# Attention through 32 packed rows, then a gated MLP: another stored order and another split of the first stage's work over the engines

## The chip, the cores and the metric

The kernel runs on one core of a Trainium2 chip. A core has five engines with their own in-order instruction queues: TensorE (PE, matmuls), VectorE (DVE), ScalarE (ACT), GpSimd (POOL) and SyncE (SP, which here only issues DMAs). The metric is the device time of one execution in microseconds, as the median of several runs.

## The reference

Eight batches, eight heads, 576 tokens of 64 features; all in fp32, with the tolerance of an fp32 result.

```python
def sm_attn(qq, kk, vv):
    s = scale * np.matmul(qq, kk.transpose(0, 1, 3, 2))
    s = s - np.max(s, axis=-1, keepdims=True)
    a = np.exp(s)
    a = a / (np.sum(a, axis=-1, keepdims=True) + 1e-09)
    return np.matmul(a, vv)
p_packed = sm_attn(p, k, v)           # 32 packed rows per head
out = sm_attn(q, p_packed, p_packed)  # every token attends to these 32 rows
...
rms = np.sqrt(np.mean(x * x, axis=-1, keepdims=True) + 1e-06)
xn = x / rms * rms_g                  # 4608 tokens x 512
g = xn @ w_gate                       # 512 -> 1536
silu = g * (1.0 / (1.0 + np.exp(-g)))
val = xn @ w_val
return (silu * val @ w_out)           # 1536 -> 512
```

## The kernel before, in words

[...] To come out at fp32 accuracy every operand is split into a high and a low fp16 part that are multiplied separately and summed in PSUM.

**The stages.** The 4608 tokens go through in 12 units of 384. For each batch, the rows p attend to k and v (stage 1: keys transposed on PE at L865 and evicted at L869, scores at L1031 and L1038, exponentials at L957, transposes evicted at L1073, packed values at L1116). Then q attends to the packed rows (queries L1426, L1431; scores L1492; softmax L1513 to L1526; the weights transposed at L1358 and split into a high part by L1378 on ACT and a low part by L1380 on DVE, the tile `aTu`). The output of attention is not formed by itself: the packed rows are multiplied into the gate and value weights ahead of time ("packed weights": L1218, L1268 and L1270 scale, L1287 multiplies, L536 and L538 split the result into the ring buffer), and L1693 multiplies `aTu` by them. That gives gate and value of a unit, 12 chunks of 128 features each. The norm's factors come as a per-chunk scale `usc` from L1668. L1729 applies silu on ACT, L1732 the product on DVE, L1744 casts the high part of the result, L1747 subtracts for the low part, both into `hall`; L1720 multiplies by w_out, and the result is evicted (L1767 on ACT, L1769 on DVE) and stored.

**The weights.** All weights are loaded once, in 12 pieces of gate and value (L614) and 6 of w_out (L673), 1 MB each, in the first 80 us, into raw buffers that are parts of `ring`, `wo` and `hall`. Each piece is taken apart into two arrays by `to_f32`: L573 on ACT makes one result; the low part is then made by L578 on POOL, L580 on ACT or L582 on DVE; L587 (or L585, where DVE made the low part) on DVE combines. The maxima for the scaling of the pieces are found by matmuls (L640 for gate/val, L691 for w_out), reduced by L645 or by L695 (DVE) or L697 (ACT), and turned into scales by L658 to L660, L720. Then w_out is split: L750 on ACT (high part), L752 on DVE (low part) and L755 (a copy of the high part).

**What sets the order.** The program is a number of generators ("chains"): keys, v, stage 1, the 18 weight pieces, queries, attention, packed weights, the MLP and so on. Each `yield` names an engine and the step's assumed cost, and each step then issues its instructions. A class `Plan` runs one step at a time in the order that the table `ORDER` (L43, 2805 numbers of chains) gives; so `ORDER` fixes the order in every engine's queue and in the DMA queue of SP. `FETCHES` (L58) is a list of assumed latencies with which TensorE's instructions are fetched; it goes into the plan's own times, by which it places filler matmuls (L1801, whose results are not used) where it thinks that PE would stand idle, and into which free buffer it takes. `BY` (L334) says by one letter per step which engine does it: A for ACT, D for DVE, P for POOL. A step that may go to several engines asks `way`:

```python
by, step = way(table, i, {"P": (POOL, 1.07, t0), "A": (ACT, act(n) + 0.06, t0), "D": (DVE2, 0.61, t1)})
yield step
if by == "P":
    nc.gpsimd.tensor_scalar(lo, lo.bitcast(U8)[..., 3::4], 1 / 32, -15.5 / 32, ALU.mult, ALU.add)
elif by == "A":
    nc.scalar.activation(lo, lo.bitcast(U8)[..., 3::4], AF.Copy, scale=1 / 32, bias=-15.5 / 32)
else:
    nc.vector.tensor_single_scalar(d, d, 3, ALU.logical_shift_left)
```

The tables of `BY` that matter here: `low` and `low_wo` (L578, L580 or L582, of the 12 and of the 6 pieces), `norm_wo` (L695 or L697), `wo_hi` (L755), `lo0` (L1747 of the first unit), `hi0` (L1744 of the first unit), `scaled` (L1643 on ACT or L1645 on DVE), `pgv` (L1268 on ACT or L1270), `keys` (L869), `a1t` (L1073).

## Time and profile before

| | before |
|---|---|
| median of 3 runs | 735.23 us (734.9 to 736.16) |
| profiled execution | 735.44 us, span 733.7 us |
| PE busy | 712.3 us (97%) |
| DVE busy | 469.6 us (64%) |
| ACT busy | 460.9 us (63%) |
| POOL busy | 138.6 us (19%) |
| granted clock of TensorE, mean | 0.991 of full speed |

The shares of the whole span are a mean over two very different parts: the first 120 us, in which the weights are loaded and taken apart while the first unit is computed, and the rest, in which the units follow each other. The page's strip of 40 slices shows the two parts; one slice is 18.3 us:

```profile
PE   8888999999999999999999999999999999999997
...
DVE  3898897788968767667657747656455553561330
ACT  4698996887797665777488477377274364461330
POOL 1235211111442242220020021020020040020110
PEclk9799999999999999999999999999999999999999
DMA  7996513677607741415734763631330333301001
```

A digit is a tenth of the slice in which the engine was busy (9 for 90% or more); PEclk is the clock granted to TensorE and DMA the share of the 16 DMA engines.

### The profile page before, as it was taken

To read this page: it belongs to the slowest core of one execution; us is meant where nothing else is said; L and a number is where in the kernel's file an instruction comes from. 1 tells how busy PE (TensorE), PEld (TensorE's weight loads), DVE (VectorE), ACT (ScalarE), POOL (GpSimd) and SP (SyncE) were. 2 spreads that over 40 slices of the span, in tenths; PEclk is the share of its full clock that TensorE was granted. 3 is DMA by queue.
4 is the path that set the end of the run, shared out by engine and by line. 5 is a ranking of instruction groups with operands and counts; after the bars stand their busy time and mean duration, and the time that the engine had idled before them with its cause. 6 is when DMAs were issued, how large, how long until landed. Compare 5 with 4: busy or idle time off the path is not lost.

```text
span 733.7 us, 19223 instructions
## 1 busy us (share of the span) xinstructions
PE 712.3 (97%) x8052; PEld 427.8 (58%) x8052; DVE 469.6 (64%) x1063; ACT 460.9 (63%) x964; POOL 138.6 (19%) x157
## 2 busy tenths in 40 slices
PE   8888999999999999999999999999999999999997
...
DVE  3898897788968767667657747656455553561330
ACT  4698996887797665777488477377274364461330
POOL 1235211111442242220020021020020040020110
PEclk9799999999999999999999999999999999999999
DMA  7996513677607741415734763631330333301001
GB/s 284 388 379 230 198 34 67 119 188 139 174 5 116 185 130 16 108 46 96 187 90 78 160 165 63 150 80 22 72 81 15 80 81 58 88 2 37 15 0 58
DMA packets 143239, 82.25 MB, mean 112 GB/s; under 512 B 105392, under 2 KB 128432, under 8 KB 143152
## 3 DMA queue, kind: packets, MB, share of 16 engines
...
q8 instruction: 63, 1.03, 0.6%
...
## 4 chain that ended last, share of the span: by engine, by line
PE 82%; DMA 7%; DVE 4%; ACT 3%; SPq 3%; issue 1%; POOL 0%; ACTq 0%; DVEq 0%
PE pm_1x L1720 12%; PE pm_3x L1693 10%; PE pm_1x L1693 9%; PE pm_2x L1693 9%; PE pm_2x L1720 9%; PE pm_0x L1693 8%; PE pm_0x L1720 8%; PE pm_3x L1720 7%; DMA wo<-in_moe_w_gate_dram 2%; DMA wo<-in_moe_w_val_dram 2%; SPq L614 2%; PE psa L1499 1%; DMA ring<-in_moe_w_out_dram 1%; PE pm_2x L1299 1%; DMA big_3x<-big_1x 1%
## 5 line engine op out<-in xcount | busy, mean ns | idle before, releaser
L1693 PEld LDWEIGHTS <-ring 128*128 128x128 f16 x2304 | 204.1, 98 | 86.0 <-issue 13.8
L1720 PEld LDWEIGHTS <-hall 128*128 128x128 f16 x1296 | 124.0, 98 | 148.5 <-issue 4.9
L1720 PE MATMUL pm_1x<-wo,hall 128*128 128x512 f16 x432 | 97.3, 379 | 0.6 <-ACT wo L755 0.6
L1747 POOL TENSOR_TENSOR hall<-t_1x,hall 128x384 f16<-128x384 f32 x44 | 41.2, 937 | 255.8 <-ACT hall L1744 250.6
L1720 PE MATMUL pm_3x<-wo,hall 128*128 128x512 f16 x288 | 64.8, 379 | 0.0
L1720 PE MATMUL pm_2x<-wo,hall 128*128 128x512 f16 x288 | 64.3, 379 | 0.0
L1720 PE MATMUL pm_0x<-wo,hall 128*128 128x512 f16 x288 | 64.1, 379 | 0.0
L1747 POOL TENSOR_TENSOR hall<-t_0x,hall 128x384 f16<-128x384 f32 x31 | 29.8, 962 | 162.9 <-ACT hall L1744 150.5
L1744 ACT CAST hall<-t_0x 128x384 f16<-128x384 f32 x69 | 35.1, 509 | 22.7 <-DVE t_0x L1732 22.4
L1693 PE MATMUL pm_3x<-aTu_1x,ring 128*128 128x192 f16 (+1 forms) x354 | 49.2, 283 | 0.0
L1693 PE MATMUL pm_1x<-aTu_0x,ring 128*128 128x192 f16 (+1 forms) x342 | 45.8, 278 | 0.3 <-ACT t_1x L1729 0.2
L1744 ACT CAST hall<-t_1x 128x384 f16<-128x384 f32 x67 | 34.0, 508 | 18.7 <-DVE t_1x L1732 18.7
L1693 PE MATMUL pm_2x<-aTu_1x,ring 128*128 128x192 f16 (+1 forms) x324 | 45.8, 284 | 0.0
L1693 PE MATMUL pm_3x<-aTu_0x,ring 128*128 128x384 f16 (+1 forms) x270 | 43.4, 301 | 1.0 <-ACT t_0x L1729 0.6
L1693 PE MATMUL pm_0x<-aTu_0x,ring 128*128 128x192 f16 (+1 forms) x276 | 38.9, 284 | 1.1 <-ACT t_1x L1729 0.9
L1693 PE MATMUL pm_0x<-aTu_1x,ring 128*128 128x192 f16 (+1 forms) x264 | 36.7, 283 | 0.0
L1693 PE MATMUL pm_2x<-aTu_0x,ring 128*128 128x192 f16 (+1 forms) x264 | 36.6, 282 | 0.0
L1693 PE MATMUL pm_1x<-aTu_1x,ring 128*128 128x384 f16 (+1 forms) x210 | 33.1, 299 | 0.0
L1747 DVE TENSOR_TENSOR hall<-t_0x,hall 128x384 f16<-128x384 f32 x42 | 24.7, 587 | 4.9 <-ACT hall L1744 4.7
L1320 POOL TENSOR_TENSOR wgv<-o_0x,wgv 128x512 f16<-128x512 f32 x14 | 16.9, 1210 | 46.8 <-ACT wgv L1318 46.8
L1729 ACT ACTIVATE t_0x<-pm_2x,usc_1x 128x384 f32<-128x384 f32 x12 | 7.0, 581 | 26.3 <-PE pm_2x L1693 23.0
L538 DVE SCALAR_TENSOR_TENSOR ring<-pm_1x,ring 128x512 f16<-128x512 f32 x24 | 16.5, 687 | 9.1 <-ACT ring L536 9.0
...
## 6 DMA issues: line engine op xcount, KB each, us to landing
...
hall<-in_moe_w_out_dram SPq DMA_DIRECT2D x4, 1024.0 KB, 10.0
wo<-in_moe_w_gate_dram SPq DMA_DIRECT2D x3, 1024.0 KB, 15.1
wo<-in_moe_w_val_dram SPq DMA_DIRECT2D x3, 1024.0 KB, 13.7
...
ring<-in_moe_w_gate_dram SPq DMA_DIRECT2D x2, 1024.0 KB, 9.1
ring<-in_moe_w_val_dram SPq DMA_DIRECT2D x2, 1024.0 KB, 12.4
```

The lines of the kernel that those rows point to most:

```text
L538: nc.vector.scalar_tensor_tensor(lo, x, s, hi, ALU.mult, ALU.subtract)
L614: nc.sync.dma_start(raw.rearrange("p k n e -> p k (n e)"), (w_gate, w_val)[n][:, 4 * c * P : 4 * (c + 1) * P].rearrange("(kt p) f -> p kt ...
L1299: nc.tensor.matmul(ps[e][32 * j : 32 * j + 32, :], pg[h, lp, j, :], wgv16[h, c, j, lw, :], start=(n3 == 0), stop=(n3 == 2),)
L1320: nc.gpsimd.tensor_tensor(wgv16[:, c, k, 1], st, wgv16[:, c, k, 0], ALU.subtract)
L1499: nc.tensor.matmul(ps2[o : o + n, i, :, pi, :], qT[:, lq, i, pi, o : o + n], packs[b][3][:, lp, pi, :, :], start=(j == 0), stop=(j == 2),)
L1693: nc.tensor.matmul(psi[:, :, o : o + n], pw[:, g, lw, w, f * P : (f + 1) * P], aT[:, :, la, g, o : o + n], start=(j == 0), stop=(j == 5),)
L1720: nc.tensor.matmul(po, hall[:, ft, lh, ts], wo[:, ft, 1 - lw, :], start=(n == 0), stop=(n == 3 * NFT - 1))
L1729: nc.scalar.activation(t, pss[0][:, :UT], AF.Silu, scale=sc[:, c, 0:1])
L1744: (nc.scalar.copy if by == "A" else nc.vector.tensor_copy)(hall[:, ft, 0, :], t)
L1747: (nc.gpsimd if by == "P" else nc.vector).tensor_tensor(hall[:, ft, 1, :], t, hall[:, ft, 0, :], ALU.subtract)
```

## The change

Three tables are replaced: `ORDER`, `FETCHES` and `BY`; no function is changed. Of the 63 entries of `FETCHES` some 50 differ; `ORDER` has the same length and differs from entry 17 on. `BY` in full, and the first entries of the other two:

```diff
-ORDER = (0, 0, 0, 0, 0, 0, 0, 0, 0, 0, 0, 0, 0, 0, 0, 0, 0, 0, 0, 0, 34, 34, 34, 35, 35, 35, 34, 1, 16,
+ORDER = (0, 0, 0, 0, 0, 0, 0, 0, 0, 0, 0, 0, 0, 0, 0, 0, 0, 16, 16, 3, 4, 3, 0, 1, 0, 0, 34, 34, 34, 35,
...
-FETCHES = (8.0, 8.0, 8.0, 8.0, 8.0, 8.0, 6.7276, 6.7063, 4.3, 4.3, 8.5735, 8.8308, 9.7613, 7.0833,
+FETCHES = (8.0, 8.0, 8.0, 8.0, 8.0, 8.0, 8.0, 4.6203, 4.3, 4.3, 9.1414, 6.3883, 7.3965, 7.163,
...
-BY = {'low': 'ADPAAAADAPAP', 'low_wo': 'APAPDP', 'pgv': 'DAPAAPDAPAAPDAPAAP', 'norm_wo': 'AADADA',
-  'keys': 'DAADADDDDADA', 'query': 'AAADDA', 'hi0': 'DADDDAADDDAD', 'lo0': 'DPDDPDDPDPPP',
-  'gv': 'PDDDPP', 'wo_hi': 'AAAAAP', 'a1t': 'DDDDAD', 'scaled': 'AAAAAA', 'store': 'DDDDDD
+BY = {'low': 'DPPPAPAAPPPP', 'low_wo': 'PPPPPP', 'pgv': 'PPDAPAPPPAAPDAPAAP', 'norm_wo': 'DDDDDD',
+  'keys': 'AADAADAAAADA', 'query': 'ADDAAA', 'hi0': 'ADDDDDADAAAA', 'lo0': 'PPPPPPPPPPPP',
+  'gv': 'DPDPPD', 'wo_hi': 'PPPPPP', 'a1t': 'DADAAA', 'scaled': 'DDADDA', 'store': 'ADDDDD
...
```

In the whole program ACT loses six L580 (9 to 3), all four L697, all five L755, four L1268 and four L1643, and gains four L869 and three L1073; DVE loses six L1747, three L1073, four L869, two L582 and others, and gains four L695 and four L1645; POOL gains eight L578 (6 to 14), six L1747, five L755 and three L1270. PE has the same matmuls in nearly the same order, with 31 fillers for 33: a run of twelve next to L647 is gone, others stand ahead of L1067, L1116 and later. In SP's queue the loads of q, of the norm's gain and of the first gate piece now stand ahead of v; the weight pieces keep their order among themselves.

Three places of the order follow. The first is POOL around the first scales `usc` (L1668). `wo_79`, `ring` and `hall` are the raw buffers: the first row is the last gate/val piece, the following L578 are w_out's. Before:

```order
L578 TENSOR_SCALAR wo_79<-wo_79 128x1024
L1668 TENSOR_SCALAR usc_0x<-gv_sc,tiny_18x 128x2
L578 TENSOR_SCALAR ring<-ring 128x1024
L1668 TENSOR_SCALAR usc_0x<-gv_sc,tiny_18x 128x2
L1270 TENSOR_TENSOR pgh_1x<-pg_0x,gv_r 128x256
L658 TENSOR_SCALAR gv_sc<-tiny_21x,gmax 128x1
L659 TENSOR_SCALAR gv_sc<-gv_r,gmax_r 128x1
L660 TENSOR_SCALAR wo_sc<-tiny_21x,gsq 128x1
L1668 TENSOR_SCALAR usc_0x<-gv_sc,tiny_18x 128x2 x2
L578 TENSOR_SCALAR hall<-hall 128x1024
L1747 TENSOR_TENSOR hall<-t_1x,hall 128x384
```

and now:

```order
L578 TENSOR_SCALAR wo_79<-wo_79 128x1024
L578 TENSOR_SCALAR hall<-hall 128x1024
L1668 TENSOR_SCALAR usc_0x<-gv_sc,tiny_19x 128x2
L658 TENSOR_SCALAR gv_sc<-tiny_21x,gmax 128x1
L659 TENSOR_SCALAR gv_sc<-gv_r,gmax_r 128x1
L660 TENSOR_SCALAR wo_sc<-tiny_21x,gsq 128x1
L578 TENSOR_SCALAR ring<-ring 128x1024
L1668 TENSOR_SCALAR usc_0x<-gv_sc,tiny_19x 128x2
L578 TENSOR_SCALAR hall<-hall 128x1024 x2
L1747 TENSOR_TENSOR hall<-t_1x,hall 128x384
L1668 TENSOR_SCALAR usc_0x<-gv_sc,tiny_19x 128x2
```

The first scales stood behind the last gate/val piece alone and now stand behind the first w_out piece too; the third stood ahead of w_out's fourth piece and now stands behind its third and fourth.

The second place is ACT between the last gate/val piece (L573 into `wgv`) and the first silu. Before:

```order
L1643 ACTIVATE e_0x<-e_0x,trio_3x 128x256 x3
L1431 COPY big_1x<-pm_0x 128x512
L1268 ACTIVATE pgh_0x<-pg_0x,gv_r 128x128 x2
L573 ACTIVATE wgv<-wo_79 128x4x256
L1378 ACTIVATE aTu_0x<-psa 128x3x256
L536 ACTIVATE ring<-pm_0x 128x512
L536 ACTIVATE ring<-pm_1x 128x512
L573 ACTIVATE wo_79<-hall 128x1024
L580 ACTIVATE hall<-hall 128x1024
L1729 ACT_TABLE_LOAD
L1729 ACTIVATE t_0x<-pm_3x,usc_0x 128x384
```

and now:

```order
L1643 ACTIVATE e_0x<-e_0x,trio_3x 128x256
L536 ACTIVATE ring<-pm_3x 128x512
L536 ACTIVATE ring<-pm_0x 128x512
L573 ACTIVATE wgv<-wo_79 128x4x256
L1378 ACTIVATE aTu_0x<-psa 128x3x256
L1431 COPY big_1x<-pm_2x 128x512
L869 COPY big_4x<-pm_3x 128x512
L536 ACTIVATE ring<-pm_0x 128x512
L573 ACTIVATE wo_79<-hall 128x1024
L869 COPY big_4x<-pm_2x 128x512
L869 COPY big_4x<-pm_3x 64x256
L536 ACTIVATE ring<-pm_1x 128x512
```

Two of the three L1643 and the L580 of w_out's first piece have left; three evictions of keys (L869) have come from DVE.

The third place is DVE around the first L1380. Before:

```order
L826 COPY pT_0x<-pm_2x 128x256
L587 SCALAR_TENSOR_TENSOR wgv<-wgv,wo_79 128x4x256
L1380 SCALAR_TENSOR_TENSOR aTu_0x<-psa,aTu_0x 128x3x256
L538 SCALAR_TENSOR_TENSOR ring<-pm_0x,ring 128x512
L869 COPY big_3x<-pm_3x 128x512
L869 COPY big_3x<-pm_2x 128x512
L869 COPY big_3x<-pm_0x 64x256
L645 TENSOR_REDUCE tiny_22x<-psb 128x2
```

and now:

```order
L1645 TENSOR_SCALAR e_0x<-e_0x,trio_3x 128x256 x2
L538 SCALAR_TENSOR_TENSOR ring<-pm_3x,ring 128x512
L538 SCALAR_TENSOR_TENSOR ring<-pm_0x,ring 128x512
L826 COPY pT_0x<-pm_1x 128x256
L587 SCALAR_TENSOR_TENSOR wgv<-wgv,wo_79 128x4x256 x2
L1380 SCALAR_TENSOR_TENSOR aTu_0x<-psa,aTu_0x 128x3x256
L538 SCALAR_TENSOR_TENSOR ring<-pm_0x,ring 128x512
L587 SCALAR_TENSOR_TENSOR wo_79<-wo_79,hall 128x1024
L645 TENSOR_REDUCE tiny_22x<-psb 128x2
```

The three L869 behind L1380 have left DVE; two L1645 stand ahead of it, and two L587 of the last gate/val pieces directly before it.

## Rows read from the trace of the kernel before

**Rows 1.** Stretches: length, busy us (instructions) of PE, PEld, DVE, ACT, POOL; clock, DMA share, GB/s.

```profile
20.00:40.00 20.00, 18.47 (x191) 13.47 (x199) 16.92 (x36) 14.91 (x18) 3.94 (x8) 0.74 1.05 386
40.00:60.00 20.00, 15.72 (x251) 10.20 (x235) 18.72 (x45) 18.81 (x38) 6.04 (x6) 0.91 1.03 379
60.00:80.00 20.00, 17.52 (x196) 11.71 (x197) 17.79 (x33) 16.43 (x28) 13.09 (x14) 1.00 0.67 239
80.00:100.00 20.00, 18.69 (x298) 12.24 (x297) 17.59 (x43) 18.47 (x34) 3.96 (x5) 1.00 0.33 90
100.00:120.00 20.00, 19.06 (x237) 9.28 (x235) 17.58 (x47) 17.62 (x39) 4.96 (x5) 1.00 0.10 20
...
140.00:734.00 594.00, 586.94 (x6381) 345.65 (x6380) 356.34 (x816) 351.60 (x771) 102.11 (x105) 1.00 0.39 88
```

**Rows 2.** PE's waits, 0 to 120 us: total us, times, longest us.

```profile
PE pm_0x L1067 <- DVE t_0x L1732: 1.2, 1, 1.2
PE psb L691 <- ACT psb L697: 1.0, 1, 1.0
PE pm_0x L1693 <- ACT t_1x L1729: 0.9, 1, 0.9
...
PE pm_1x L1720 <- ACT wo L755: 0.6, 1, 0.6
...
PE pm_3x L1693 <- ACT t_0x L1729: 0.6, 1, 0.6
...
PE psb L1116 <- DMA big_3x<-in_v_dram: 0.4, 1, 0.4
```

**Rows 3.** DVE in order of time: start us, us, line, operation, [idle before <-releaser].

```profile
51.85 1.78 DVE L587 SCALAR_TENSOR_TENSOR wgv<-wgv,wo 128x1024 uint32<-128x1024 uint32 x1
...
56.66 1.23 DVE L587 SCALAR_TENSOR_TENSOR wgv<-wgv,wo 128x1024 uint32<-128x1024 uint32 x1 [0.43 <-issue]
57.80 0.95 DVE L1380 SCALAR_TENSOR_TENSOR aTu_0x<-psa,aTu_0x 128x768 f16<-128x768 f32 x1
...
59.26 0.68 DVE L869 COPY big_3x<-pm_3x 128x512 f32<-128x512 f32 x1
```

**Rows 4.** ACT in order of time, from the softmax's last scaling to the first silu.

```profile
53.13 1.30 ACT L1643 ACTIVATE e_0x<-e_0x,trio_3x 128x256 f32<-128x256 f32 x3
...
55.39 1.18 ACT L573 ACTIVATE wgv<-wo 128x1024 f32<-128x1024 f32 x1
56.47 0.80 ACT L1378 ACTIVATE aTu_0x<-psa 128x768 f16<-128x768 f32 x1
...
61.22 1.28 ACT L1729 ACT_TABLE_LOAD   x1 [0.92 <-DVE tiny_22x L645]
```

**Rows 5.** POOL in order of time, 44 to 80 us.

```profile
51.43 1.13 POOL L578 TENSOR_SCALAR wo<-wo 128x1024 uint32<-128x1024 uint8 x1 [3.82 <-DMA wo<-in_moe_w_val_dram]
...
59.65 1.11 POOL L578 TENSOR_SCALAR ring<-ring 128x1024 uint32<-128x1024 uint8 x1 [5.86 <-DMA ring<-in_moe_w_out_dram]
60.86 1.63 POOL L1668 TENSOR_SCALAR usc_0x<-gv_sc,tiny_18x 128x2 f32<-128x2 f32 x1
...
67.58 2.19 POOL L578 TENSOR_SCALAR hall<-hall 128x1024 uint32<-128x1024 uint8 x1
...
77.11 2.63 POOL L578 TENSOR_SCALAR hall<-hall 128x1024 uint32<-128x1024 uint8 x1 [3.96 <-DMA hall<-in_moe_w_out_dram]
```

**Rows 6.** Groups on ACT, 0 to 130 us: count | busy us, mean ns | idle before.

```profile
L580 ACT ACTIVATE wo<-wo 128x1024 uint32<-128x1024 uint8 x4 | 4.6, 1145 | 0.0
...
L755 ACT COPY wo<-o_1x 128x1024 f16<-128x1024 f16 x3 | 3.1, 1043 | 0.0
```

**Rows 7.** PE at the first gate matmul.

```profile
60.00 0.50 PE L1693 MATMUL pm_3x<-aTu_0x,ring 128*128 128x384 f16 x2 [0.19 <-DVE big_3x L869]
```

**Rows 8.** SP's issue of w_out's first piece, and the DMA issues' median us to landing.

```profile
45.57 0.39 SPq L673 DMA_DIRECT2D hall<-in_moe_w_out_dram  x1
...
hall<-in_moe_w_out_dram SPq DMA_DIRECT2D x4, 1024.0 KB, 10.0
```

More of the change, by code (lines that the diff above doesn't have):

```diff
@@ L57 @@
 FETCH = 4.3
-FETCHES = (8.0, 8.0, 8.0, 8.0, 8.0, 8.0, 6.7276, 6.7063, 4.3, 4.3, 8.5735, 8.8308, 9.7613, 7.0833, 6.652, 9.2881, 11.2118, 11.101, 9.0986, 5.0836, 4.3, 6.826, 9.1123, 7.2529, 8.9496, 6.817, 4.3, 7.2194, 5.4815, 5.4589, 4.3, 4.3, 12.5384, 10.4012, 5.85, 4.3, 7.2196, 11.2844, 6.652, 10.6036, 4.3, 4.3, 9.3832, 5.0917, 7.1847, 4.3, 4.3, 4.3, 6.8544, 8.6891, 5.5852, 4.3, 8.995, 4.6413, 4.687, 4.3, 4.3, 5.0414, 4.3, 4.3, 6.2857, 4.3, 4.3)
+FETCHES = (8.0, 8.0, 8.0, 8.0, 8.0, 8.0, 8.0, 4.6203, 4.3, 4.3, 9.1414, 6.3883, 7.3965, 7.163, 7.2878, 8.1005, 11.3553, 11.577, 11.4766, 4.3, 4.3, 9.0249, 10.6493, 6.0211, 6.9708, 6.9336, 4.3, 11.5226, 6.221, 5.776, 4.3, 4.3, 13.3077, 9.5193, 4.5178, 4.3, 7.2415, 12.2214, 9.2315, 7.6025, 4.3, 4.3, 7.1177, 6.723, 6.6415, 4.3, 4.3, 4.3, 5.2008, 8.3238, 4.3902, 4.3, 5.3658, 6.6851, 4.9147, 4.3, 4.3, 4.6087, 4.3, 4.3, 6.3191, 4.3, 4.3)
 FETCH_AT, FETCH_NEED, FETCH_SIZE = 128, 449, 256
```

4 lines of the change are left out of this document (2 added, 2 removed).

## The prediction

> **What bounds the kernel now.** I read four views, in this order. The first is the table of stretches [rows 1]. From 140 us to the end TensorE (PE) is busy for 586.94 of 594.00 us at full clock: that part, four fifths of the time, is bound by its matmuls, and a microsecond won before it stays won to the end. From 40 to 120 us it is otherwise. VectorE (DVE) is busy 17.6 to 18.7 of each 20 us, ScalarE (ACT) 16.4 to 18.8, GpSimd (POOL) 4 to 13, while PE reaches 15.7 to 19.1, part of it at a reduced clock (0.91 in 40 to 60). The summed idle time of PE in the four rows from 40 to 120 is 4.28 + 2.48 + 1.31 + 0.94 = 9.0 us. The loads take the DMA engines' whole time up to 60 us (share 1.05 and 1.03) and 0.67 of it in the stretch after. So two engines are nearly full, one is nearly idle, and PE waits.
>
> The second view, PE's waits up to 120 us [rows 2], says for whom: a maximum reduction or copy on DVE (L1067 1.2 us), ScalarE's norm eviction (L691 behind L697, 1.0), its silu (L1693 behind L1729, 0.9 and 0.6), its copy of the split of w_out (L1720 behind L755, 0.6). The third view is the order in time around the first gate matmul [rows 3, 4]. L1380 on DVE, which makes the last operand of that matmul, runs from 57.80 to 58.75, directly behind L587 of the last gate/val piece (56.66), which begins 0.1 us after ACT's L573 for it (55.39 to 56.57) has ended; ACT for its part has L1643 at 53.13 and L1378 at 56.47. ACT runs its queue without a gap here, DVE with one of 0.43 us: work taken out of the queues ahead brings that matmul forward. The fourth is POOL's order [rows 5], for the place where the work goes.
>
> **The change part by part.** It changes no arithmetic and no tile size; it exchanges engines and reorders queues. Counted from the instruction order, ahead of the first L1378 ACT loses four of seven L580 (1.145 us each [rows 6]: -4.6), two of three L1643 (1.30 us for three: -0.9) and some evictions, some of these against gained ones of L869 and L1073: about 6 us less in all. Ahead of L1380 DVE loses an L582, an L1073, one set of L658 to L660 and two L869, and gains two L1645 and one small L869. At the 0.68 of L869 [rows 3] for each of the four that go (the set as one) that is -2.7; the three that come are a half of that size or less, at 0.25 to 0.34 some +0.8: net about -2.0. DVE is then the one that decides, with less relief.
>
> *Term one, the first gate matmul.* DVE's -2.0 is the lower estimate, because the copies that left were early ones, from a time when DVE idled, and others were moved into that time. In the stretch directly ahead of L1380 the work that is gone is up to 4.0 us; but nothing at all comes forward if the load of the last piece holds L587. Its POOL part started at 51.43 after 3.82 us of waiting for the load [rows 5], so it is in at 51.4, and L587 needs a L573 (1.18 [rows 4]) and a POOL L578 (1.13) beside it: not before 52.6, against 56.66. The load leaves 4.0 us. Behind L1380 the L869 of 59.26 and two more leave DVE as well; the first L1693 began at 60.00 [rows 7], in their midst. Between 0 and -4.0, I take -2.5, nearer to the counted -2.0.
>
> *Term two, the waits of 60 to 120 us.* Through the first down-projection ACT loses four L697, five L755 (1.04 each [rows 6]) and two L580 of w_out, and DVE its low parts L1747. The named waits are 1.2 + 1.0 + 0.9 + 0.6 + 0.6 = 4.3 us [rows 2]. Three of them stand behind an instruction that the change takes from ACT (L697 twice: itself and, in the queue, just ahead of the silu of the 0.9; L755 once): 2.5 us. The others depend on the length of DVE's queue. Not all goes: PE's next wait is that of a silu or a product L1732 whose matmul came earlier too. Between 0 and -4.3, I take -2.3.
>
> *Price one, POOL.* 22 large instructions go to POOL in the first 125 us, by count: eight L578, six L1747, five L755, three L1270. On POOL nothing waits ahead of them, but DVE can be slowed. The L587 at 51.85, during which POOL ran L578 and L1668, took 1.78 us, the one at 56.66, with POOL idle, 1.23 [rows 3, 5]: 0.55 for such a meeting. POOL suffers as well: L578 took 1.11 to 1.13 twice and 2.19 and 2.63 twice [rows 5]. Ahead of the first gate matmul there are six more L578. If none meets a DVE instruction of that kind the price is 0, if every one does 6 x 0.55 = +3.3. I take +0.7: of the four rows of L578 shown, one had such a meeting with an L587 on the shown DVE rows, so 6 x 0.25 x 0.55 = 0.8, rounded down because a part of it falls in DVE's waits. Later, 16 x 0.25 x 0.55 = 2.2 us of DVE's time is less than the 5 to 6 us that it is relieved of there: no charge on the path.
>
> The Trainium skill, "SBUF — State Buffer", section "Who interferes with whom", speaks against this part: a DVE instruction with two SBUF inputs and a GpSimd instruction that reads SBUF hold an exclusive lock against each other, and the later one fully blocks. By it every meeting would cost up to the whole rest of the other instruction, and the price could stand at its upper end, +3.3, the sum at -1.2 and the time at 734.0. The 0.55 us above fits a lock that was held for most of the rest of an L578; how often they meet no row here shows.
>
> *Price two, the loads.* In SyncE's queue q, g and the first weight piece now stand ahead of v. That is 0.26 MB plus small ones ahead of v's second half, at the 386 GB/s of 20 to 40 us [rows 1] 0.7 us, at the most 0.9. PE did wait for that half (L1116, 0.4 us [rows 2]), so the packed values come up to 0.9 later. Most is caught by DVE and ACT, which have other pieces to convert meanwhile: between 0 and +0.9, I take +0.3.
>
> *Fillers.* The twelve L1801 matmuls in one run near L647 go, others come: 33 become 31. The clock averaged 0.74 in 20 to 40 us although they were there [rows 1]; PE there waits for loads and DVE. Charged at nothing, with ±0.5 for the clock.
>
> Sum: -2.5 - 2.3 + 0.7 + 0.3 = **-3.8 us**, made against the profiled execution's 735.44, so 731.6; that execution lies 0.2 above the median of 735.23, so I forecast **731.4 us**.
>
> **The rivals.**
>
> *All of it comes.* Term one at -4.0, term two at -4.3, the prices near 0: 8 us, 727.0. For it speaks that ACT loses as much as 10 us; against it that PE's order is nearly the same and something else then ends its waits. Chance 0.14 for more than 6 us.
>
> *The gain is given back at the down-projection.* It needs w_out, whose last piece started on POOL at 77.11 after 3.96 us of waiting for its load [rows 5]; that load is not earlier after the change. From there L587, the norm (L691, L695), the scale and six splits on DVE follow in line. If this chain, not PE's order, sets the first L1720, the earlier first gate matmul only makes PE wait longer ahead of it. Left is half of the 1.0 + 0.6 us at L691 and L755 and less than 0.5 elsewhere, minus the prices of 1.0: about 0, 735.1. For it: the DMA engines are full up to 60 us. Against it: in 80 to 100 and 100 to 120 PE is busy 18.69 and 19.06 of 20 us, so it has other work while the chain runs. Chance 0.18 for within 0.2%, which is about 1.5 us and what a measurement of this kernel can tell from no change.
>
> *POOL becomes the bound, and it gets slower.* The scales L1668 that ACT's silu needs stand in POOL's queue behind L578 of all six w_out pieces; before, behind three. The first stands behind that of w_out's first piece, issued at 45.57 and landed some 10.0 us later [rows 8], 55.6: with 1.11 + 1.63 us it is there at 58.3, in time for a silu at 58.5 to 60 (before, its table load ended at 62.50 [rows 4]). The third stands behind the fourth piece; before, that L578 began at 67.58, so 67.58 + 2.19 + one L1747 + one L1668, some 71.3, while term one would have the silu that it serves 2.5 us earlier than before: hardly any slack is left. If the L578 there run at 2.19 to 2.63 instead of 1.11 (the same collision as in price one), the six take 6.5 to 9 us more, the later L1668 are 3 to 5 us late, and PE waits for as much: -2.5 (term one) + 5 = +2.5, 737.7. It decides from the point where the mean L578 between 55 and 80 us is over about 2 us. For it: two of the four L578 shown are. Against it: the two that ran long did so without PE's waiting for POOL. Chance 0.16. The lock of the section named under price one would be the cause of such lengths.
>
> That the change doesn't do what it says can be excluded for the engines: the order shows each moved instruction.
>
> **How the numbers follow.** The forecast (1.5 to 6 us faster) has 0.52, all of it 0.14, given back 0.18, slower 0.16: faster 0.66, same 0.18, slower 0.16. The range of 726.8 to 737.4 takes in the full terms (727.0) and most of the slower case; its forecast part alone is 729.2 to 733.7.
>
> **What would show it.** Right: L1380 at 55 to 56 instead of 57.80, the first L1693 at 57 to 58 instead of 60.00 [rows 7]; the waits behind L697 and L755 gone; ACT and DVE each some 8 to 12 us less busy, POOL some 21 to 26 more; PE's idle time from 40 to 120 us about 6 instead of 9. Term one wrong: L1380 at 57 or later. Term two wrong: the same idle time under other names. The given-back case: an earlier first L1693 and an L1720 at the same time as before. The slower case: PE's waits for L1729 behind POOL's L1668, and L578 of over 2 us. Wrong altogether would be a change that arises after 140 us, where I see none.

## The result, and the profile after

| | before | changed |
|---|---|---|
| median | 735.57 us (734.9 to 736.16) | **739.32 us** (739.25 to 740.58) |
| ratio of the means | | 1.0055, 95% interval 1.0038 to 1.0073 |
| profiled execution, its span | 735.44, 733.7 us | 740.58, 738.8 us |

The change is slower by 3.75 us, outside the range of 726.8 to 737.4; four runs each. The profiled execution is the slowest of the changed kernel's four, so its trace shows a larger loss than the medians. The busy time of ScalarE moved as forecast (460.9 to 451.5 us) and that of GpSimd nearly (138.6 to 158.6, 20.0 more where 21 to 26 were forecast), but not that of VectorE (469.6 to 470.8, forecast 8 to 12 less). From the page of the changed kernel:

```profile
PE 713.4 (97%) x8047; PEld 429.7 (58%) x8050; DVE 470.8 (64%) x1052; ACT 451.5 (61%) x947; POOL 158.6 (21%) x179
```

The stretches of the changed kernel, with the columns of [rows 1]:

```profile
20.00:40.00 20.00, 15.22 (x177) 12.07 (x161) 15.12 (x31) 11.90 (x18) 6.49 (x9) 0.74 1.01 369
40.00:60.00 20.00, 15.97 (x257) 11.76 (x255) 16.76 (x43) 15.77 (x32) 12.08 (x14) 0.83 1.05 385
60.00:80.00 20.00, 18.28 (x231) 12.29 (x233) 19.66 (x31) 16.90 (x27) 13.18 (x14) 1.00 0.62 219
80.00:100.00 20.00, 18.31 (x319) 12.32 (x304) 17.09 (x44) 16.29 (x31) 10.32 (x14) 1.00 0.44 132
100.00:120.00 20.00, 18.20 (x233) 9.12 (x232) 18.48 (x34) 15.11 (x30) 8.48 (x9) 1.00 0.01 2
```

ScalarE is relieved in every row but that of 60 to 80 us (16.43 before, 16.90 now), and PE's idle time from 40 to 120 us is what it was: 4.03 + 1.72 + 1.69 + 1.80 = 9.2 us, 9.0 before. From 20 to 40 us PE is 3.2 us less busy, but that is no work lost: the filler matmuls (L1801) there took 6.49 us before and 3.12 now. PE's waits up to 120 us in the changed kernel, as in [rows 2]; the first line is the longest wait of the kernel before, which stands ahead of the lines of [rows 2] and isn't among them:

```profile
PE pm_0x L647 <- DVE tiny_15x L645: 2.5, 1, 2.5
```
```profile
PE psb L1358 <- DVE e_0x L1526: 2.0, 2, 1.1
PE pm_0x L647 <- DVE tiny_15x L645: 1.8, 1, 1.8
PE pm_1x L1181 <- ACT junk_0x L1148: 1.6, 1, 1.6
PE pm_0x L865 <- DMA big_2x<-in_k_dram: 1.6, 1, 1.6
...
PE psb L691 <- DVE wo_ss L695: 1.0, 1, 1.0
PE pm_1x L865 <- DVE ring L538: 0.8, 1, 0.8
PE pm_0x L1693 <- DVE ring L538: 0.8, 1, 0.8
PE pm_2x L1720 <- POOL wo L755: 0.8, 1, 0.8
```

The waits that the prediction named are there under other names: L691 waits 1.0 us for L695 on VectorE instead of L697 on ScalarE, L1720 0.8 for the same copy L755 on another engine (0.6 before). Those for silu and the 1.2 us at L1067 are gone; waits for L538 have grown (two of 0.8, one of 0.4 before) and those for the softmax's L1526 too (2.0, 0.3 before).

The first gate matmul, on PE, VectorE and GpSimd of the changed kernel (start us, us), against [rows 3, 7]:

```profile
63.92 1.14 PE L1693 MATMUL pm_0x<-aTu_0x,ring 128*128 128x384 f16 x6 [0.83 <-DVE ring L538]
```
```profile
59.30 3.10 DVE L587 SCALAR_TENSOR_TENSOR wgv<-wgv,wo 128x1024 uint32<-128x1024 uint32 x2
62.33 0.94 DVE L1380 SCALAR_TENSOR_TENSOR aTu_0x<-psa,aTu_0x 128x768 f16<-128x768 f32 x1
63.19 0.67 DVE L538 SCALAR_TENSOR_TENSOR ring<-pm_0x,ring 128x512 f16<-128x512 f32 x1
```
```profile
59.04 1.14 POOL L578 TENSOR_SCALAR hall<-hall 128x1024 uint32<-128x1024 uint8 x1
60.28 2.21 POOL L1668 TENSOR_SCALAR usc_0x<-gv_sc,tiny_19x 128x2 f32<-128x2 f32 x1
```

L1380 comes at 62.33 instead of 57.80, the first L1693 at 63.92 instead of 60.00 (its weights were loaded at 62.88, the time that the expectations below go by). The two L587 ahead of L1380 took 3.10 us beside two GpSimd instructions; alone one takes 1.23 [rows 3]. In both kernels the matmul starts with the end of the instruction behind L1380 that, by the names, reads the PSUM buffer it writes: L869 from pm_3x before (59.26 + 0.68 = 59.94, [rows 3, 7]), L538 from pm_0x now (63.86). L1380, from which the prediction counted, had ended 1.2 and 0.6 us sooner.

### The profile page after: what moved, and what is told of

It is laid out like the page before. It is cut to its first block, busy times and chain, and to the rows that moved or that the text cites. A ratio compares the mean times of both kernels' runs of the same rounds, so it can differ in the third digit from the quotient of the medians.

```text
span 738.8 us, 19234 instructions
## 1 busy us (share of the span) xinstructions
PE 713.4 (97%) x8047; PEld 429.7 (58%) x8050; DVE 470.8 (64%) x1052; ACT 451.5 (61%) x947; POOL 158.6 (21%) x179
## 3 DMA queue, kind: packets, MB, share of 16 engines
q8 instruction: 63, 1.03, 0.6%
## 4 chain that ended last, share of the span: by engine, by line
PE 79%; DVE 8%; DMA 5%; ACT 3%; SPq 2%; issue 2%; POOL 1%; DVEq 0%; ACTq 0%; POOLq 0%
PE pm_3x L1720 12%; PE pm_3x L1693 9%; PE pm_2x L1720 9%; PE pm_2x L1693 8%; PE pm_0x L1693 8%; PE pm_1x L1693 8%; PE pm_1x L1720 6%; PE pm_0x L1720 5%; DMA ring<-in_moe_w_val_dram 2%; PE psa L1499 1%; PE pm_2x L1299 1%; DVE ring L538 1%; DMA big_5x<-big_4x 1%; PE pm_0x L1299 1%; PE psb L1130 1%
## 5 line engine op out<-in xcount | busy, mean ns | idle before, releaser
L1693 PEld LDWEIGHTS <-ring 128*128 128x128 f16 x2304 | 204.2, 98 | 86.4 <-issue 14.4
L1720 PEld LDWEIGHTS <-hall 128*128 128x128 f16 x1296 | 124.0, 98 | 148.2 <-issue 5.1
L1720 PE MATMUL pm_3x<-wo,hall 128*128 128x512 f16 x468 | 104.9, 379 | 0.0
L1747 POOL TENSOR_TENSOR hall<-t_0x,hall 128x384 f16<-128x384 f32 x50 | 46.3, 926 | 270.9 <-ACT hall L1744 269.2
L1720 PE MATMUL pm_2x<-wo,hall 128*128 128x512 f16 x360 | 80.8, 379 | 0.8 <-POOL wo L755 0.8
L1747 POOL TENSOR_TENSOR hall<-t_1x,hall 128x384 f16<-128x384 f32 x31 | 30.0, 968 | 135.7 <-ACT hall L1744 128.7
L1720 PE MATMUL pm_0x<-wo,hall 128*128 128x512 f16 x252 | 56.9, 379 | 0.0
L1720 PE MATMUL pm_1x<-wo,hall 128*128 128x512 f16 x216 | 48.3, 379 | 0.0
L1693 PE MATMUL pm_3x<-aTu_1x,ring 128*128 128x384 f16 (+1 forms) x294 | 43.5, 290 | 0.2 <-DVE o_1x L1769 0.2
L1693 PE MATMUL pm_3x<-aTu_0x,ring 128*128 128x384 f16 (+1 forms) x300 | 43.5, 288 | 0.0
L1693 PE MATMUL pm_2x<-aTu_1x,ring 128*128 128x192 f16 (+1 forms) x306 | 43.5, 285 | 0.0
L1693 PE MATMUL pm_0x<-aTu_0x,ring 128*128 128x384 f16 (+1 forms) x282 | 42.3, 292 | 1.0 <-DVE ring L538 0.8
L1744 ACT CAST hall<-t_1x 128x384 f16<-128x384 f32 x66 | 33.5, 508 | 15.6 <-DVE t_1x L1732 15.1
L1693 PE MATMUL pm_1x<-aTu_0x,ring 128*128 128x192 f16 (+1 forms) x300 | 41.3, 281 | 0.2 <-ACT t_0x L1729 0.2
L1693 PE MATMUL pm_1x<-aTu_1x,ring 128*128 128x192 f16 (+1 forms) x300 | 40.1, 278 | 0.0
L1693 PE MATMUL pm_2x<-aTu_0x,ring 128*128 128x192 f16 (+1 forms) x270 | 37.8, 283 | 0.4 <-DVE o_1x L1769 0.4
L1693 PE MATMUL pm_0x<-aTu_1x,ring 128*128 128x384 f16 (+1 forms) x252 | 37.7, 292 | 0.0
L1320 POOL TENSOR_TENSOR wgv<-o_1x,wgv 128x512 f16<-128x512 f32 x16 | 18.9, 1179 | 34.0 <-ACT wgv L1318 33.9
L538 DVE SCALAR_TENSOR_TENSOR ring<-pm_0x,ring 128x512 f16<-128x512 f32 x29 | 19.8, 684 | 5.6 <-ACT ring L536 5.6
L1747 DVE TENSOR_TENSOR hall<-t_1x,hall 128x384 f16<-128x384 f32 x38 | 21.0, 552 | 3.7 <-ACT hall L1744 3.6
```

The costliest lines, as they stand in the source:

```text
L538: nc.vector.scalar_tensor_tensor(lo, x, s, hi, ALU.mult, ALU.subtract)
L1320: nc.gpsimd.tensor_tensor(wgv16[:, c, k, 1], st, wgv16[:, c, k, 0], ALU.subtract)
L1693: nc.tensor.matmul(psi[:, :, o : o + n], pw[:, g, lw, w, f * P : (f + 1) * P], aT[:, :, la, g, o : o + n], start=(j == 0), stop=(j == 5),)
L1720: nc.tensor.matmul(po, hall[:, ft, lh, ts], wo[:, ft, 1 - lw, :], start=(n == 0), stop=(n == 3 * NFT - 1))
L1744: (nc.scalar.copy if by == "A" else nc.vector.tensor_copy)(hall[:, ft, 0, :], t)
L1747: (nc.gpsimd if by == "P" else nc.vector).tensor_tensor(hall[:, ft, 1, :], t, hall[:, ft, 0, :], ALU.subtract)
```

## The experiments

The theories at the outset: the late start (loads and the waits at L865 and L1181) is the cause; or GpSimd's holding of VectorE is; or single steps that now stand behind the wrong work. Later runs asked where the loss lies, and whether the order or the engines make it.

Each step keeps the fillers that it has in the kernel that its place comes from. BEFORE and AFTER stand for the two tables ORDER; `until(X, chain, n)` are the entries of X ahead of the n-th step of a chain, `rest(X)` those not yet taken, in X's order. In such a hybrid every letter of BY is that of the kernel from which its step was taken; FETCHES is that of the kernel that stands last, and no run changes it alone. The step mlp 1 is the first gate matmul; attention 5 is the first unit's L1358, and attention 26, 28 and 30 are the second unit's scores, its exp and its L1358. Each group of runs timed the kernel before beside it (medians 735.07 to 735.80). One trace scatters by up to 2 us in the first 60 us (h1 and g1 below have the same program up to the first L1693 and show it at 61.73 and 59.83; the part on the clock below says why), so verdicts go by medians.

### The start

e1 puts the first loads back into the old order: v (chain 1) in two halves around q (16) and the first weight piece (4), the norm's gain (3) last.

```diff
-ORDER = (0, 0, 16, 16, 3, 4, 3, 0, 1, 0, 0, 34, 34,
+ORDER = (0, 0, 1, 16, 16, 4, 1, 3, 3, 0, 0, 0, 34, 34,
...
```

> The changed kernel with one edit: SyncE's first loads stand as in the kernel before (v's first half, q, the first gate piece, v's second half, then the norm's gain; in the changed kernel q, gain and gate piece stand ahead of v). The number and the places of the filler matmuls are held at those of the changed kernel. Theory A, the start: in the changed kernel the keys' second half came 1.6 us later (PE's wait for it at L865) and the packed values 2.2 us later, and the first maximum of unit 0 (L1513) at 29.2 instead of 25.2; by it this edit takes back about 2 of these 4 us, L1513 at 27, L865 without that wait, and 1.5 to 2 us in all: 737.5 to 738. Theory B, contention between DVE and POOL (DVE's time over its shortest durations went from 2.9 to 11.0 us up to 140 us): the start is caught up by other waits, and the time stays within 0.7 us of the changed kernel's 739.3.

Measured: 738.13 us (737.27 to 740.51), ratio 1.0040 (1.0026 to 1.0054). The wait at L865 went and the first unit's softmax (L1513) came 1.1 us earlier, 28.17 (25.16 before); L1380 stayed at 62.41. e3 adds to it that L573 and L578 of the second weight piece go behind ScalarE's L1148, L1166 and L1171, and PE's L1181 behind the scores L1492 (on its own that gave 740.20):

```diff
 e3, from e1:
-ORDER = (..., 5, 5, ..., 2, 2, 2, 6, 6, 17,
+ORDER = (..., 5, 5, ..., 6, 6, 17, 2, 2, 2,
...
```

> Both of the edits before together: loads and the two queue places of the start as in the kernel before, all else as changed. Theory A: L1513 at 26 instead of 29.2, the first gate matmul L1693 at 60 to 61 instead of 62.9, and 2.5 to 3 us of the 4 taken back: 736.3 to 736.8. Theory B: under 1 us, 738.3 or more; L1693 is moved, but the loss of 100 to 130 us (2.8 us in the changed kernel) grows by as much.

Measured: 740.10 us, 1.0055 (1.0043 to 1.0067); L1513 at 27.71, L1380 at 62.45. A softmax that is 1.5 us earlier moves nothing at the first gate matmul. The theory that the start alone holds the loss falls; whether the loads' order is worth e1's 1.2 us stays unclear, since the intervals of e1 and the change overlap.

### Engines and order apart

e5: the old order with the new engines. e8: the new order with the old engines for the low parts and the copies.

```diff
 e5: ORDER = BEFORE
+BY = that of the changed kernel
 e8: ORDER = AFTER
-'low': 'DPPPAPAAPPPP', 'low_wo': 'PPPPPP', 'lo0': 'PPPPPPPPPPPP', 'wo_hi': 'PPPPPP'
+'low': 'ADPAAAADAPAP', 'low_wo': 'APAPDP', 'lo0': 'DPDDPDDPDPPP', 'wo_hi': 'AAAAAP'
```

> The kernel before, its order, its fillers, with the changed kernel's table of engines alone. The prediction's premise was that ACT's and DVE's relief of some 12 and 8 us brings the first gate matmul forward. If engine relief is worth what it said, 732 to 734. If the contention of POOL and DVE (8 us more of DVE time in the changed kernel) eats it, 735 to 738. If order and engines only fit each other, as the reverse run suggests (the four tables back in the changed order: 756), 740 to 755, with PE waiting for POOL's queue.

> The changed kernel's order with the choice of engine as before for four tables: the low parts of the weight pieces (L578 on POOL 14 to 6, the others back on ACT and DVE), the low parts L1747 of unit 0 and the copies L755. Fillers as in the changed kernel. Theory B: DVE's excess falls from 11 to about 4 us, more than the 6 us of work that DVE gets back are worth, and ACT has idle time enough for its 12 us: 2 to 3 us faster than the changed kernel, 736.3 to 737.3. Theory A: the contention is in idle time mostly; ACT and DVE get back work in stretches where the order has no room for it: 0 to 3 us slower, 739.3 to 742.

Measured: e5 743.94 us, 1.0113 (1.0100 to 1.0127); e8 756.24, 1.0279 (1.0264 to 1.0293). The new engines, in the order made for the old ones, cost 8 us; taking a part of GpSimd's new work away again, in the order that was made for it, costs 17 more than the change. Order and engines belong together, and what they do to each other is larger than every term of the prediction.

### Single suspects

e9 moves one L578 (that of piece 8; VectorE waited 1.01 us for it, until 45.76) to VectorE; e11 moves the second unit's exp (L1518) and L1521 to L1526 ahead of the fifth piece of the split of w_out, of a silu and its product:

```diff
 e9:
-'low': 'DPPPAPAAPPPP'
+'low': 'DPPPAPAADPPP'
 e11, names for numbers:
-ORDER = (... wo_split 3, mlp, wo_split 3, wo_split 4, ..., attention, mlp, attention, wo_split 3,
+ORDER = (... wo_split 3, attention, mlp, wo_split 3, attention, wo_split 4, ..., mlp, wo_split 3,
...
```

> The changed kernel with one letter of the table changed: the low part of the ninth weight piece is made by DVE (L582, 0.69 us) instead of by POOL (L578). Taking the start back had moved L1513 by 1.5 us and the first gate matmul by nothing, so another chain sets that. Theory C, POOL holds up DVE and PE's clock falls: in the changed kernel L578 of this piece began at 43.8 and took 1.97 us beside DVE's work, DVE's L587 waited 1.0 us for it, PE stood idle 1.8 us ahead of L647, and then ran L1426 and L640 at a granted clock of 0.68 (49 to 54 us). By it the L587 ends 1.5 to 2 us earlier, the clock in 49 to 54 is above 0.8, the first gate matmul comes at 60 to 61.5 instead of 62.9, and the time falls by 1 to 2.5 us: 736.8 to 738.3. Rival, the amount of DVE's work: 0.7 us more on DVE, no gain: 739.3 or up to 0.7 more.

> The changed kernel with two steps of unit 1's softmax moved ahead: the exponential L1518 on ACT stands behind one L750 instead of behind three and a silu, and L1521 to L1526 on DVE behind two L752 fewer. PE's order is the same. Theory D, the second loss (between 100 and 130 us the changed kernel falls from 2.5 to 5.3 us behind the kernel before, L1526 of unit 1 from +0.7 at L1513 to +3.1): L1526 comes at 106.5 to 107.5 instead of 109.5, unit 1's first gate matmul at 132 to 133 instead of 134.8, the time 1.5 to 2.5 us less than the changed kernel: 736.8 to 737.8. Rival: the splits that are put back delay L1720 by as much, and PE waits there: no change, 738.8 to 739.8.

Measured: e9 740.83 us, 1.0062 (1.0050 to 1.0075); e11 742.37, 1.0084 (1.0070 to 1.0098). In e11 L1526 came at 105.39, 4 us earlier than in the change, and L1606 behind it at 120.40 (120.74 in the change); PE now waited 2.6 us for L1729 behind the exp. All of these edits together gave 741.44. The place of the exp is not the cause by itself. e9 leaves its theory open, because the edit did not do what it was to do: L582 took 1.61 us beside another L578 instead of 0.69, so that VectorE's combination of the piece ended at 47.30 instead of 46.99, no sooner, and the granted clock was at 1.2 GHz from 48.1 to 54.7 us:

```profile
44.42 1.61 DVE L582 TENSOR_SCALAR wgv<-wgv 128x1024 uint32<-128x1024 uint32 x1
```

### Two halves

h1 is the old kernel up to the first gate matmul and the change behind it, h2 the other way round.

```diff
-ORDER = AFTER
+h1: ORDER = until(BEFORE, mlp, 1) + rest(AFTER)
+h2: ORDER = until(AFTER, mlp, 1) + rest(BEFORE)
```

> Steps up to the first gate matmul in the order and on the engines of the kernel before, every later step of the first stage in the changed kernel's order and on its engines. Two losses (mine): the 2.9 us lost up to the first gate matmul and the 2 to 3 us lost between 80 and 130 us are independent, one in each part. Then the first gate matmul comes at about 60.0 us as before, PE loses 2 to 3 us more than before between 80 and 130 us, and the median is 737.5 to 738.5. Rival, one cause: the later loss only follows from the late first part; then the median is 735 to 736, as before. Rival, whole tables: an order is good only together with its own start; then it is above 741.

> The other half: the changed order and engines up to the first gate matmul, then the order and engines of the kernel before. Two losses: first gate matmul at about 62.9 us, little lost after it, median 737.5 to 738.7. One cause: what comes late at the start costs again later, median 739 to 740.5. Whole tables: above 741.

Measured: h1 736.61 us (735.57 to 737.78), 1.0018 (1.0009 to 1.0027), +1.4; h2 738.13 (737.84 to 739.79), 1.0045 (1.0032 to 1.0059), +2.9. The sum, 4.3, is the change's 3.75 within the intervals. So there are two losses that do not need each other, the second smaller than I expected (737.5 to 738.5).

### The first loss

g4 takes only the start from the change (up to the first unit's L1358), g5 only the middle (from there to the first gate matmul).

```diff
+g4: ORDER = until(AFTER, attention, 5) + rest(BEFORE)
+g5: ORDER = until(BEFORE, attention, 5) + until(AFTER, mlp, 1) + rest(BEFORE)
```

> The changed order and engines only up to the first unit's L1358 (the start, with its loads and the 4 us later softmax), before from there on. If the start costs the first part's 2.9 us: 737.5 to 738.5. If the start's delay is hidden and 36 to 62 us cost it: 735 to 736.

> The counterpart of g4_front: the kernel before up to the first unit's L1358, the changed order and engines from there to the first gate matmul, before after that. If the first part's 2.9 us come from the start alone: first gate matmul at 58 to 60 us and a median of 734 to 735.6, since the changed middle made up 1.5 us in h2. If the middle (36 to 62 us) costs as well: first gate matmul at 61 to 62 us, 736.5 to 738. If the parts do not fit: above 738.

Measured: g4 743.28 us, 1.0107 (1.0094 to 1.0121); g5 740.10, 1.0073 (1.0060 to 1.0086). In g4 the softmax's L1526 is 3.2 us late and the first gate matmul 4.4 (64.44). Another 3 us are lost in its trace after 250 us: PE stands idle for 1.75 us ahead of L1579 at 272.00, ended by nothing that the profile names, and then runs at 1.2 GHz instead of 2.4 until 276 us:

```profile
273.00:276.20 3.20, 3.20 (x12) 1.47 (x10) 0.54 (x2) 1.88 (x5) 1.30 (x2) 0.50 0.69 223
276.40:300.00 23.60, 23.34 (x202) 12.85 (x201) 15.36 (x42) 15.38 (x41) 7.51 (x8) 1.00 0.03 6
```

In g5 the softmax is in time (31.80), and the middle loses as much by itself; PE's longest wait from 30 to 60 us there is for a product that the change gave to GpSimd:

```profile
PE pm_3x L1287 <- POOL pgh_0x L1270: 2.9, 1, 2.9
```

Neither half of the first part is faster than the old one, and each is worse beside the other kernel's half than beside its own. Both fit badly with what stands beside them, so neither time is the price of its piece, and which step of the first part holds the loss is left open.

### The second loss

In h1 the second unit's steps come like this on VectorE and ScalarE:

```profile
110.63 0.41 DVE L1372 TENSOR_SCALAR aT_0x<-psb 128x256 f32<-128x256 f32 x1
...
114.28 0.14 DVE L1555 COPY tiny_43x<-sv 64x1 f32<-64x1 f32 x1
...
118.24 0.16 DVE L1606 TENSOR_TENSOR trio_4x<-s_1x 128x3 f32<-128x3 f32 x1 [0.42 <-ACT psb L1589]
```
```profile
114.52 0.45 ACT L1589 ACTIVATE psa<-psa,tiny_43x 128x256 f32<-128x256 f32 x1 [0.61 <-DVE tiny_43x L1555]
```

L1555 stands 3.6 us behind L1372, behind L1453 and L538 of other chains, and L1589 on ScalarE waits for it. g1 puts that step directly behind L1372; g2 leaves it and moves L755 back to ScalarE:

```diff
 g1, from h1:
-ORDER = (... attention (L1372), ..., query, attention (L1555),
+ORDER = (... attention (L1372), attention (L1555), ..., query,
...
 g2, from h1:
-'wo_hi': 'PPPPPP'
+'wo_hi': 'AAAAAP'
```

> As h1_before_first (before up to the first gate matmul, the change after it), but the second unit's step with the copies L1553 and L1555 stands directly behind its L1372 on VectorE, as in the kernel before, no longer behind a piece of the output weights, L1453, and two combinations of L538. Order theory: the second unit's L1589 waits for nothing else, so L1589 starts 2 to 3 us earlier, L1606 comes at 115 to 116 us (118.24 there), the waits of PE at L1618 and L1358 behind it (0.7 and 0.4) go, and the median falls by 0.5 to 1 us, to 735.6 to 736.1. Contention theory: the pieces of VectorE that GpSimd stretches set this stretch; the step gains on its own chain and nothing at the end, 736.3 to 737.

> As h1_before_first, but the copies L755 of the output weights stand on ScalarE as in the kernel before (five of six), the order unchanged. Contention theory: without the GpSimd copies beside them the pieces L752 take 1.28 us each and L1526 0.96, VectorE's excess from 80 to 120 us falls from 4.7 to about 2.5, and the median falls to 735.2 to 736, though ScalarE has 5.2 us more. Order theory: ScalarE's exp and L1729 now stand behind 1.04 us copies at places chosen without them; 737 to 738.5.

Measured: g1 735.72 us, 1.0007 (0.9996 to 1.0017); g2 737.51, 1.0026 (1.0015 to 1.0037). One step's place moves the median by 0.9 of the 1.4 us; since the intervals of h1 and g1 overlap, that is likely and not shown. In the traces the way from L1526 to L1606 shrinks by 0.7 us (11.2 to 10.5), less than I expected. With fewer GpSimd copies the kernel is slower, not faster, although VectorE's instructions stretched by GpSimd fell from 13 to 9 up to 135 us. Here the contention theory falls, and the order theory fits.

g3 lets the old kernel take over again ahead of the second unit's scores, g6 behind its L1515, g7 behind its L1526:

```diff
+g3: ORDER = until(BEFORE, mlp, 1) + until(AFTER, attention, 26) + rest(BEFORE)
+g6: ORDER = until(BEFORE, mlp, 1) + until(AFTER, attention, 28) + rest(BEFORE)
+g7: ORDER = until(BEFORE, mlp, 1) + until(AFTER, attention, 30) + rest(BEFORE)
```

> Three parts: before up to the first gate matmul, the change from there to the second unit's L1498, before from there on. If the change gains between 60 and 90 us (in the trace of h1 the 48th gate matmul after the first came 1.8 us sooner behind the first than before) and gives it back between 100 and 130: median 733.7 to 734.7, below both kernels. If that gain is only the trace's, since the first gate matmul came late there: 735.2 to 736. If the parts do not fit: above 737.

> As g3_mid, but the kernel before takes over only ahead of the second unit's exp, so that L1513 and L1515 of that unit keep the place they have in the change (98 to 99 us; in g3 101.24). Latency theory: after 98 us the second unit's softmax chain is the bound, and TensorE being early gives nothing unless that chain is early too; here it is, with the old tail behind it: L1526 at 104.5 to 105.5, L1606 at 112 to 113.5, median 733.5 to 734.8. If ScalarE's queue (L1729, L755, the table load) sets it instead: as g3, 735 to 735.6.

> As g6, but the kernel before takes over ahead of the second unit's L1358, behind L1526. Latency theory: L1526 as in g1 (106.0), then the old tail (7.6 us to L1606): L1606 at 113.6 to 114.5, the end as before or up to 0.6 us sooner, 734.6 to 735.5. Order theory of g1 alone (only the place of L1553 and L1555 mattered): as g1, 735.5 to 736.

Start times in us in one profiled execution each (of L1720 that of its first weight load), and the medians:

| | first L1693 | first L1720 | unit 1: L1513 | L1526 | L1606 | median |
|---|---|---|---|---|---|---|
| before | 60.00 | 99.09 | 101.05 | 106.35 | 113.94 | 735.07 to 735.80 |
| changed | 63.92 | 101.62 | 101.79 | 109.49 | 120.74 | 739.32 |
| h1 | 61.73 | 99.13 | 99.30 | 107.00 | 118.24 | 736.61 |
| g1 | 59.83 | 98.18 | 98.34 | 106.04 | 116.55 | 735.72 |
| g3 | 60.51 | 97.97 | 101.24 | 106.54 | 114.12 | 735.22 |
| g7 | 59.88 | 97.31 | 97.52 | 105.22 | 114.78 | 735.26 |
| **g6** | 59.56 | 97.90 | 98.07 | 105.22 | 112.95 | **733.78** |

g3 is at 1.0002 (0.9993 to 1.0011), g7 at 1.0000 (0.9991 to 1.0009), **g6 at 0.9982 (0.9973 to 0.9991), 1.4 us faster than the kernel before** and the fastest of the study. The second part of the change does gain: the first L1720 comes 0.9 to 1.8 us sooner in g1, g3, g6 and g7 (counted from the first L1693, 0.7 to 1.7 us). In g3 the gain ends in one wait, which was 0.6 us in [rows 2]:

```profile
PE pm_2x L1720 <- ACT wo L755: 1.9, 1, 1.9
```

Behind the first L1720 PE runs out of other work, and the second unit's chain on VectorE and ScalarE sets the time: early scores (g6: L1513 at 98.07) with the old tail behind them keep the gain, as g6's expectation said of L1526, L1606 and the median. In g6 that tail is

```profile
108.22 0.42 DVE L1372 TENSOR_SCALAR aT_0x<-psb 128x256 f32<-128x256 f32 x1
...
108.83 0.14 DVE L1555 COPY tiny_40x<-sv 64x1 f32<-64x1 f32 x1
...
112.95 0.16 DVE L1606 TENSOR_TENSOR trio_4x<-s_1x 128x3 f32<-128x3 f32 x1 [0.48 <-ACT psb L1589]
```

L1526 to L1606 takes 7.7 us in g6, 7.6 before, 11.2 in h1 and in the change. In g7 it takes 9.6 with the same tail. In its one trace the chain goes over PE, which ran at 1.2 GHz from 107.5 to 110.7 us: L1287's matmuls took 0.63 us each instead of 0.38, and ScalarE waited 2.6 us for them.

```profile
107.50:110.70 3.20, 3.20 (x44) 0.91 (x47) 2.32 (x7) 0.60 (x1) 1.04 (x1) 0.50 0.00 0
```

Last, g8 gives a copy that stands behind the exp on ScalarE in g6 to GpSimd:

```diff
-'wo_hi': 'PPPAAP'
+'wo_hi': 'PPPPAP'
```

> As g6_l1513, with one more copy of the output weights (the fourth L755, 1.03 us, on ScalarE behind the exp) on GpSimd. TensorE's longest wait between 62 and 140 us that an edit can take there, 1.1 us at L1720 behind that copy, goes. Latency theory: L1526 (105.22 to 106.18) still releases the second unit's L1358, so the wait comes back at L1358 as 1.0 to 1.5 us, L1606 stays at 112.5 to 113.3 and the median within 0.6 us of g6: 733.3 to 734.4. If that wait were a cost of its own: 732.4 to 733.0.

Measured: 733.95 us, 0.9982 (0.9973 to 0.9991), L1606 at 112.95 as in g6. The wait did not go; the copy took 2.03 us on GpSimd instead of 1.03, and PE waited 1.5 us for it:

```profile
PE pm_2x L1720 <- POOL wo L755: 1.5, 1, 1.5
```
```profile
102.40 2.03 POOL L755 COPY wo<-o_0x 128x1024 f16<-128x1024 f16 x1
```

So the wait was not taken away, as the run was meant to; it grew from 1.1 us in g6 to 1.5, and that cost nothing (733.95 and 733.78). g8 also speaks against the clock as the cause of the gain: its trace is at 1.2 GHz from about 21 to 31 and 45 to 48 us like that of the kernel before, and its span is 1.5 us shorter (732.2, 733.7).

## Why the prediction was wrong

**Term one, the first gate matmul: -2.5 forecast, +3.9 in the trace, +2.9 in the time (h2).** The step that failed is "work taken out of the queues ahead brings that matmul forward". VectorE's rows from the start to its L1380, before and after (columns of [rows 1], the third busy time is VectorE's), each behind the row up to the softmax's last step L1526:

```profile
0.00:32.14 32.14, 27.04 (x349) 18.74 (x350) 18.23 (x42) 16.58 (x26) 6.92 (x22) 0.84 0.90 329
0.00:57.80 57.80, 48.64 (x711) 33.30 (x711) 42.25 (x97) 40.63 (x71) 12.61 (x27) 0.88 0.97 353
```
```profile
0.00:35.75 35.75, 28.71 (x388) 20.60 (x391) 19.20 (x43) 14.81 (x25) 9.47 (x23) 0.86 0.94 329
0.00:62.33 62.33, 50.19 (x712) 36.05 (x715) 42.54 (x93) 36.67 (x64) 23.79 (x38) 0.86 0.96 342
```

VectorE is busy 42.54 us ahead of L1380, 0.3 more than before, where I counted 2.0 less: the count was about right (four instructions fewer), but five of them took 3.2 us longer beside GpSimd, and one before had taken 0.6 longer. The larger part is idle time: 62.33 - 42.54 = 19.8 against 57.80 - 42.25 = 15.6. Of these 4.2 us, 2.6 lie ahead of L1526 (16.55 against 13.91) and 1.6 between L1526 and L1380. I had read that ScalarE ran without a gap and VectorE almost so; that was true of the old order, and I took it over into the new one. Between L1526 and L1380 VectorE now waits three times: 1.0 us for an L578 (of 1.97 us), 1.3 for PE's L1618 and 0.5 for its L647. That this idle time is the loss is read from one trace: g4 and g5 fit it, but in e3 L1526 came 1.5 us sooner and L1380 did not. Which wait holds the first loss stays open.

**Term two, the waits of 60 to 120 us: -2.3 forecast, 0 in the trace.** The failed step is to take a wait's length as the price of the instruction it is named after. Three of the waits were to go with instructions taken from ScalarE; L691 and L1720 wait as long for the same work on another engine, and those of silu went but others came (5.2 us of idle time from 60 to 120 us, 4.7 before). The text had this as "the same idle time under other names". The wait at L1067 was for a product (L1732), not for "a maximum reduction or copy". Up to 98 us the second part does gain 0.9 to 1.8 us (g1, g3, g6, g7), less than the 2.3 I took; it is given back behind that.

**Price one, GpSimd: the size of a meeting was right, their number not.** Up to 135 us 18 VectorE instructions of the changed kernel are lengthened by more than 0.25 us against their usual time (the time that a tenth of the instructions of the same form stays under, over all traces), each with a GpSimd instruction running beside it, 10.9 us in all or 0.60 each (I took 0.55); before there are 5, 2.4 us. These 8.5 us more are about what VectorE's busy time lacks of the forecast. I expected 22 x 0.25 = 5 or 6 more; there are 13 more. The trace so agrees with the Trainium skill, "SBUF — State Buffer", section "Who interferes with whom", on a full block (two of them end within 0.03 us of the GpSimd instruction, shown at the end). Ahead of the first gate matmul it is 2.6 us more than before where I took 0.7, and 1.2 of them, at L1645 and L587, stand between 56.37 us and L1380, where VectorE has no gap over 0.15 us, so that L1380 is later by them. Over the whole kernel the lengthened time does not set the loss: g6 has 11 such instructions (6.3 us) and is faster than the kernel before, e8 has 7 (3.9 us) and is 20 us slower. What the contention costs in the first loss no run separates; g2 tested it in the second alone.

**Price two, the loads: 0 to 0.9 forecast; the first unit's softmax came 4.1 us late** (L1513 29.25 against 25.16). I costed the bytes ahead of v and not what stands behind them in the queues: PE's L1181 waits 1.6 us for L1148 with the scores L1492 behind it, and ScalarE's L573 of the second piece, which waits for its load, has L1148 behind it. e1 and e3 took back 1.1 and 1.5 us at L1513, which gained nothing at L1380.

**The order itself was priced at nothing.** I argued that PE's order was nearly the same and costed exchanges of engines one by one. e5 and e8 show 8 and 20 us for the same exchanges in an order not made for them; g1 points to some 0.9 for one step's place. That is the main gap: of a change that is an order I priced only the engines.

**The rivals.** The slower case was right in sign alone. Its mechanism needed L578 of over 2 us between 55 and 80 us and PE's waits for silu behind L1668; the six L578 there took 1.11 to 1.17 us and no such wait exists. The case of the gain given back at the down-projection comes nearest for the second part: the gain is given back there, though not because w_out's chain sets the first L1720 (behind the old first part that comes earlier), but because the second unit's chain sets what follows. My term against it, that PE has other work from 80 to 120 us, holds only up to the first L1720.

**Fillers and clock, charged at nothing.** The granted clock from 40 to 60 us is 0.83 instead of 0.91 [rows 1]: PE runs at the lower of its two levels (1.2 instead of 2.4 GHz) in two stretches, 44.1 to 47.3 and 50.9 to 54.2 us, instead of one, 45.2 to 48.4. L1618, for which VectorE waits 1.3 us, lies in the second. What such a stretch costs is seen in h1 and g1, one program up to there:

```profile
45.20:51.80 6.60, 6.17 (x69) 4.17 (x69) 5.14 (x17) 6.15 (x14) 1.31 (x2) 0.50 1.06 364
```
```profile
45.60:48.80 3.20, 3.20 (x43) 2.04 (x29) 2.62 (x7) 2.57 (x7) 0.96 (x2) 0.50 1.07 380
49.00:52.00 3.00, 2.89 (x64) 2.12 (x62) 2.87 (x12) 2.38 (x4) 0.00 (x0) 1.00 1.06 345
```

In h1 the clock stays low to 51.8 us, in g1 it is full from 49; the first unit's L1606 is 0.65 us apart (46.66 and 46.01), the first gate matmul 1.90. By that about 1.3 us of the 3.9 in the trace may be the clock's, an estimate from two traces. It is not the loss as a whole: h2's trace is at 1.2 GHz for about as long as that of the kernel before (some 13 us up to 60) and its span is 2.6 us longer (736.3, 733.7); and the one run of the change with a mean granted clock of 0.992 took 739.25 us, while 19 runs of the kernel before with that clock took 735.3 in the mean.
